# Hash attention and channel mix on one core: the projection load and two head loads change their DMA queues

## The chip, the cores and the metric

The kernel runs on one core of a Trainium2 chip. The metric is the device time of one execution in microseconds. Before the change the median of three runs is 248.6 us (248.2 to 249.51).

## The reference

The inputs are q, k and v (4 batches, 8 heads, 768 positions, 64 features, all float32), a projection of 64 x 6, and the weights of a channel mix. What is computed, cut to what matters:

```python
q_bits = (einsum('bhsd,dk->bhsk', q, proj) > 0)      # 6 bits for each position
k_bits = (einsum('bhsd,dk->bhsk', k, proj) > 0)
mask = q_bucket[:, :, :, None] == k_bucket[:, :, None, :]
scores = where(mask, q @ k.T / 8, -1e9)
attn = softmax(scores) @ v                           # x: [4, 768, 512] over all heads
xk = mu_k * x + (1 - mu_k) * x_prev                  # x_prev: x one position earlier
xr = mu_r * x + (1 - mu_r) * x_prev
out = sigmoid(xr @ w_r) * (relu(xk @ w_k)**2 @ w_v)
```

## The kernel before

The 32 heads are worked on as 16 pairs. For every pair there are 12 slots: 2 heads by 6 blocks of 128 keys. In a slot TensorE makes the scores of one key block against 768 queries (`score`, L484), ScalarE takes the exponential (L498), and two slots later TensorE multiplies it with the values (`pv`, L514). The bucket mask is put into the score as six extra rows of the operands: the signs of the projected q and k, written into `aq` and `ak` beside the 64 features. Between the score and the values of each slot stand the channel mix's matmuls of an earlier batch, and the preparation of later pairs. The whole order is written out by hand, with a table of work by pair and slot (`WORK`, `FETCH`); every engine carries out its own instructions in that order.

The start is what the change touches. It runs in this order in the code:

- L69: the projection (64 rows of 6 numbers, 1.5 KB) is loaded by GpSimd, ahead of the identities (`make_identity`) and of GpSimd's memsets (L221). L230 copies it on GpSimd to a second place, into partitions 64 to 127, when it has landed.
- `load_qk(0)` (L249 to L260) loads q and k of the first pair, one head at a time: head 0's q from SyncE, its k from ScalarE, then head 1's q from SyncE and k from ScalarE, 192 KB each.
- L955 and L956: a small activation on ScalarE, with which the activation table is loaded.
- From SyncE, in this order: v of head 0 (192 KB), q and k of pair 1 (`load_qk(1)`, L262, 384 KB each), two small loads of `mu_rows` (L960), v of head 1, v of pair 1, q and k of pair 2. The semaphores of loads are used again in turn, so that a later load on SyncE waits for one some eight loads earlier to land.
- `keep_warm(9, ...)` (L970): nine matmuls without use for the result.
- `turn_pe` (L326): three transposes on TensorE into a PSUM bank, then a copy to `t32` by VectorE (L333) or ScalarE (L335). The order on TensorE is: q of head 0, k of head 0, k of head 1 (L985, L986, L989), then the bit matmuls of head 0 (`bits_first`, L363; they need the projection, also its second place), q of head 1 (L994), q of pair 1's head 0 (L998), then the first score.
- `cast_pe` (L341) writes the features of q and k as bf16 into `aq` and `ak`, halves on VectorE, GpSimd and ScalarE. `signs_first` (L370) writes the signs: of q on ScalarE (L374), of k on VectorE (L403).
- Head 1's bit matmuls (`bits_of_second`) come in slot 0, after the first score.

Of the kernel before, what the change touches and what calls it, by code (L numbers as in the profile page):

```python
# [36 lines left out]
def kernel(  # L37
# [13 lines left out]
    nc = tc.nc  # L51
    B, H, S, D = q.shape
    NB = proj.shape[1]
# [10 lines left out]
    consts = ctx.enter_context(tc.tile_pool(name="consts", bufs=1))  # L64

    projp = consts.tile([P, 64], FP32, name="projp")
    nc.gpsimd.dma_start(out=projp[0:D, 0:NB], in_=proj)  # L69
    ident32 = consts.tile([P, P], FP32, name="ident32")  # L70
    make_identity(nc, ident32)
    ident16 = consts.tile([P, P], BF16, name="ident16")
# [99 lines left out]
    def fast():  # L172
        with ExitStack() as fx:
# [75 lines left out]
            def load_qk(n):  # L249
                b, t = divmod(n, NPB)  # L250
                tl = nat.tile([P, 2, 2, HALF], FP32, name=f"qk{n}", tag="qk")
                nats[n] = tl
                if n == 0:
                    for j in range(2):
                        for i, eng in enumerate((nc.sync, nc.scalar)):
                            eng.dma_start(  # L256
                                out=tl[:, i, j, :],
                                in_=SRC[i][b, 2 * t + j].rearrange("(p c) d -> p (c d)", c=NC_),
                            )
                    return  # L260
                for i in range(2):
                    nc.sync.dma_start(  # L262
                        out=tl[:, i, :, :],
                        in_=SRC[i][b, 2 * t : 2 * t + 2].rearrange(
                            "j (p c) d -> p j (c d)", c=NC_
                        ),
                    )
# [18 lines left out]
            def load_pair(n, sides="qk"):  # L286
                if n < NTE:
                    load_qk(n)
                else:
                    load_blocks(n, sides)  # L290
# [660 lines left out]


            load_qk(0)
            warm = rcp.tile([P, 1], FP32, name="warm", tag="warm")
            nc.vector.memset(warm, 0.0)  # L955
            nc.scalar.activation(warm, warm, AF.Exp)  # L956
            load_v(0, (0,))
            load_qk(1)
            for x, src in enumerate((moe_mu_k, moe_mu_r)):
                nc.sync.dma_start(  # L960
                    out=mu_rows[x * NDC : (x + 1) * NDC, :],
                    in_=src.rearrange("(c p) -> c p", p=P),
# [317 lines left out]
```

## Time and profile before

| | |
|---|---|
| median of 3 runs | 248.6 us |
| the profiled execution's own time | 248.52 us |
| its span, first to last instruction | 246.3 us |
| TensorE matmuls busy | 240.4 us, 98% |
| ScalarE busy | 208.4 us, 85% |
| VectorE busy | 176.5 us, 72% |
| GpSimd busy | 115.5 us, 47% |
| data moved by DMA | 36.70 MB |

Lines in the profile name the kernel's line (L331), the engine, the operation, what it writes and reads, and how many of them. PE is a matmul on TensorE, PEld a weight load on it, DVE VectorE, ACT ScalarE, POOL GpSimd, SP SyncE; a q behind the name means the engine's queue, where DMAs are issued. In a timeline the first column is the start in us, the second the length, and the bracket at the end says how long the engine was idle before and what ended that. Lines of stretches give, after the window, the busy time of each engine, then the granted clock of TensorE, the busy share of the DMA engines, and GB/s.

### The profile page before, as it was taken

Reading aid. Unit: us, or ns where it says so; the run is one execution under the profiler, and the core shown is the slowest. Engines: PE = TensorE matmul, PEld = TensorE weight load, DVE = VectorE, ACT = ScalarE, POOL = GpSimd, SP = SyncE. Lnnn points to the kernel's source line nnn. Section 1 sums busy time; section 2 is a strip of 40 time slices with the busy share of each in tenths; the row PEclk is TensorE's granted clock in tenths of the full one; section 3 lists DMA queues with packets and bytes.
Section 4 is the critical chain, followed back from the end, with each engine's and each line's share of the span. In section 5 each row is a group of like instructions: output and inputs, shape, how many; then the busy total and the mean of one; then the engine's idle time right before and its main releaser. Section 6 shows DMA issues by size and latency. Waiting matters only on the chain.

```text
span 246.3 us, 6710 instructions
## 1 busy us (share of the span) xinstructions
PE 240.4 (98%) x2443; PEld 145.6 (59%) x2443; DVE 176.5 (72%) x415; ACT 208.4 (85%) x344; POOL 115.5 (47%) x216
## 2 busy tenths in 40 slices
PE   8999999999999999999999999999999999999995
PEld 5566766665656556565665556565665656555443
DVE  2877887878887948586696957586696838499522
ACT  4898999999999989889999988889999999629620
POOL 6889786797637190835528091744619000000000
PEclk9999999999999999999999999999999999999999
DMA  6979888496999383956929475865920111120133
GB/s 219 373 173 243 175 192 195 80 224 166 201 205 232 108 199 97 271 119 207 185 72 212 106 197 134 244 134 173 214 71 5 48 45 43 45 86 3 43 115 107
DMA packets 28230, 36.70 MB, mean 149 GB/s; under 512 B 3216, under 2 KB 25376, under 8 KB 28192
## 3 DMA queue, kind: packets, MB, share of 16 engines
q1 hardware_dynamic: 25744, 33.21, 51.3%
q0 software_dynamic: 2160, 2.62, 7.0%
q8 instruction: 20, 0.33, 0.6%
q10 hardware_dynamic: 288, 0.39, 0.5%
q14 instruction: 18, 0.15, 0.2%
HBM read 31.99 MB, written 6.29 MB: 155 GB/s over the span
## 4 chain that ended last, share of the span: by engine, by line
PE 87%; ACT 7%; DMA 2%; issue 1%; SPq 1%; DVE 0%; ACTq 0%
PE sc L491 23%; PE vp L620 17%; PE kp L620 16%; PE oo L528 12%; PE rp L620 8%; ACT pt L498 6%; PE bb L450 3%; DMA qk<-in_q_dram 2%; PE ot L575 2%; PE tp L331 2%; PE oo L519 1%; PE bb L423 1%; ACT sq L314 1%; ACT kr L651 0%; SPq L256 0%
## 5 line engine op out<-in xcount | busy, mean ns | idle before, releaser
L498 ACT ACTIVATE pt<-sc 128x768 bf16<-128x768 f32 x192 | 151.1, 815 | 15.0 <-PE sc L491 12.4
L491 PE MATMUL sc<-aq,ak 70*128 70x384 bf16 (+1 forms) x384 | 93.8, 325 | 1.2 <-ACT pt L498 0.5
L528 PEld LDWEIGHTS <-pt 128*128 128x128 bf16 x1152 | 60.6, 97 | 27.0 <-ACT pt L498 0.2
L528 PE MATMUL oo<-va,pt 128*128 128x65 bf16 x1152 | 66.3, 193 | 0.0
L620 PE MATMUL vp<-wv_sb,k 128*128 128x512 bf16 (+1 forms) x200 | 54.4, 370 | 0.0
L620 PE MATMUL kp<-xk,wk_sb 128*128 128x384 bf16 x256 | 52.8, 326 | 0.2 <-ACT kr L651 0.2
L491 PEld LDWEIGHTS <-ak 70*128 70x128 bf16 (+1 forms) x384 | 34.3, 98 | 27.0 <-issue 4.6
L393 POOL TENSOR_SCALAR aq<-t 64x768 bf16<-64x768 f32 x24 | 19.9, 829 | 59.9 <-DVE t L388 45.8
L657 DVE TENSOR_TENSOR k<-kr 128x384 bf16<-128x384 bf16 x64 | 28.7, 458 | 11.7 <-ACT kr L651 11.2
L620 PEld LDWEIGHTS <-wk_sb 128*128 128x128 bf16 x256 | 21.6, 97 | 13.6 <-issue 3.8
L651 ACT ACTIVATE kr<-kp 128x384 bf16<-128x384 f32 x50 | 25.0, 499 | 4.5 <-PE kp L620 4.5
L620 PE MATMUL rp<-wr_sb,xr 128*128 128x512 bf16 x96 | 27.7, 379 | 0.0
L678 DVE SCALAR_TENSOR_TENSOR os<-th,vp 128x512 f32<-128x512 bf16 (+1 forms) x25 | 16.5, 661 | 15.0 <-PE vp L620 13.0
L620 PEld LDWEIGHTS <-k 128*128 128x128 bf16 x200 | 16.8, 97 | 10.8 <-issue 1.2
L668 ACT ACTIVATE th<-rp 128x512 bf16<-128x512 f32 x24 | 14.3, 595 | 9.8 <-PE rp L620 9.8
L388 DVE STREAM_TRANSPOSE t<-bl 128x768 f32<-128x768 f32 x24 | 22.3, 955 | 0.0
L393 POOL TENSOR_SCALAR ak<-t 64x768 bf16<-64x768 f32 x24 | 20.2, 840 | 4.3 <-DVE t L388 1.4
L479 POOL TENSOR_TENSOR s<-vf 128x192 f32<-128x192 f32 x32 | 20.7, 648 | 0.0
L314 ACT ACTIVATE sq<-bl 128x768 bf16<-128x768 f32 x24 | 20.2, 843 | 0.0
L576 DVE COPY xt<-ot 128x768 bf16<-128x768 bf16 x16 | 8.9, 558 | 14.3 <-PE ot L575 14.3
L477 POOL CAST va<-vf 128x384 bf16<-128x384 f32 x32 | 17.5, 548 | 2.5 <-DMA vf<-in_v_dram 1.6
L541 DVE TENSOR_TENSOR su<-oo,vb 128x390 f32<-128x390 f32 x12 | 6.7, 561 | 10.0 <-PE oo L528 10.0
(87 smaller groups left out, 238.5 us busy)
## 6 DMA issues: line engine op xcount, KB each, us to landing
bl<-in_q_dram SPq DMA_DIRECT2D x48, 176.0 KB
bl<-in_k_dram SPq DMA_DIRECT2D x48, 176.0 KB
vf<-in_v_dram SPq DMA_DIRECT2D x15, 384.0 KB
out_dram<-os SPq DMA_DIRECT2D x18, 256.0 KB
out_dram<-os SPq DMA_DIRECT2D x12, 128.0 KB
qk<-in_q_dram SPq DMA_DIRECT2D x3, 384.0 KB
qk<-in_k_dram SPq DMA_DIRECT2D x3, 384.0 KB
wk_sb<-in_moe_w_k_dram POOLq DMA_DIRECT2D x2, 512.0 KB, 6.9
```

The costliest lines, as they stand in the source:

```text
L314: nc.scalar.activation(junk, src, AF.Square, accum_out=acc)
L388: nc.vector.transpose(t32(n)[:, i].rearrange("p h (c f x) -> p (h c) f x", c=3, f=4), src)
L393: eng.tensor_scalar(out=augs[n % NSET]["qk"[i], j][ROWS[j], :], in0=t32(n)[ROWS[j], i].rearrange("p h y -> p (h y)"), scalar1=(1.0, ALPHA)[i],
L477: nc.gpsimd.tensor_copy(to, of)
L479: nc.gpsimd.tensor_add(s3, vf[:, 0 : 3 * D], vf[:, 3 * D : 6 * D])
L491: nc.tensor.matmul(sc[:, sp, 0:HALF], au["k", j][kr, jc * P : (jc + 1) * P], au["q", j][kr, sp * HALF : (sp + 1) * HALF], start=True, stop ...
L498: nc.scalar.activation(pt.rearrange("p (s q) -> p s q", s=2), sc[:, :, 0:HALF], AF.Exp, bias=EXP_BIAS, scale=SCALE / 2.0 if (n, j) == TWIC ...
L528: nc.tensor.matmul(oo[:, ic, :], pts[n, j, jc][:, ic * P : (ic + 1) * P], vas[n % NSET][j][:, jc, :],  start=(late(n) and jc == 0 and ic = ...
L620: nc.tensor.matmul(box["t"], lhs(), rhs(), start=(i == 0), stop=(i == len(mms) - 1))
L651: nc.scalar.activation(kr, kp, AF.Relu)
L657: 1, lambda: nc.vector.tensor_tensor(out=k2, in0=kr, in1=kr, op=ALU.mult)
L678: nc.vector.scalar_tensor_tensor(out=box["os"][:, y], in0=box["th"][:, y], scalar=1.0, in1=vp, op0=ALU.add, op1=ALU.mult,)
```

## The change

The projection is loaded by ScalarE, as its first load, and no longer by GpSimd. The loads of head 1 of the first pair change places: ScalarE loads its q and SyncE its k. Head 0 stays as it is, but its k is now ScalarE's second load. No other line changes; what is computed is the same.

```diff
     projp = consts.tile([P, 64], FP32, name="projp")
-    nc.gpsimd.dma_start(out=projp[0:D, 0:NB], in_=proj)
+    nc.scalar.dma_start(out=projp[0:D, 0:NB], in_=proj)
     ident32 = consts.tile([P, P], FP32, name="ident32")
...
                 if n == 0:
                     for j in range(2):
-                        for i, eng in enumerate((nc.sync, nc.scalar)):
+                        for i, eng in enumerate(((nc.sync, nc.scalar), (nc.scalar, nc.sync))[j]):
                             eng.dma_start(
                                 out=tl[:, i, j, :],
                                 in_=SRC[i][b, 2 * t + j].rearrange("(p c) d -> p (c d)", c=NC_),
```

## The prediction

> **What bounds the kernel now.** I read the page first: busy times and the chain that ended last.
>
> ```profile
> PE 240.4 (98%) x2443; PEld 145.6 (59%) x2443; DVE 176.5 (72%) x415; ACT 208.4 (85%) x344; POOL 115.5 (47%) x216
> PE 87%; ACT 7%; DMA 2%; issue 1%; SPq 1%; DVE 0%; ACTq 0%
> ```
>
> The end is set by TensorE's in-order stream, with some ScalarE exponentials in it. The 2% of DMA is one stretch at the very start, and the change touches only the start. So I opened the chain in order of time for the first 9 us.
>
> ```profile
> 2.13 5.59 DMA qk<-in_q_dram
> 7.72 0.14 issue
> 7.86 0.52 PE tp L331 x3
> 8.37 0.33 PE sc L491 x2
> ```
>
> Nothing before 7.72 us is TensorE work on this chain. TensorE waits for q of the second pair (`load_qk(1)`), whose turn (L998) stands ahead of the first score in program order. From 7.86 us on the chain is TensorE and ScalarE, with no DMA to hold it at a fixed time. So whatever moves the first score moves the end by the same amount, unless something else gets in first. The timeline gives the order of the start.
>
> ```profile
> 0.74 0.90 ACTq L256 DMA_DIRECT2D qk<-in_k_dram  x2
> 0.74 0.87 SPq L256 DMA_DIRECT2D qk<-in_q_dram  x2
> 1.28 0.74 POOL L69 DMA_DIRECT2D projp<-in_proj_dram  x1 [0.84 <-POOLq L1264]
> 1.67 1.28 ACT L956 ACT_TABLE_LOAD   x1 [1.67 <-PEq L1264]
> 2.96 0.20 ACT L956 ACTIVATE warm<-warm 128x1 f32<-128x1 f32 x1
> 3.64 0.92 PEld L331 LDWEIGHTS tp<-ident,qk 128*128 128x128 f32 x4 [0.23 <-issue]
> 4.79 0.48 ACT L335 COPY t<-tp 128x384 f32<-128x384 f32 x1 [1.62 <-PE tp L331]
> 5.31 0.39 POOL L230 COPY projp<-projp 64x6 f32<-64x6 f32 x1 [0.92 <-DMA projp<-in_proj_dram]
> 5.43 0.48 ACT L335 COPY t<-tp 128x384 f32<-128x384 f32 x1 [0.16 <-PE tp L331]
> 6.00 0.10 PEld L363 LDWEIGHTS bf0q<-t,projp 64*32 64x32 f32 x1 [0.17 <-issue]
> 6.78 0.55 PE L331 MATMUL tp<-ident,qk 128*128 128x128 f32 x3
> 6.95 0.99 ACT L374 ACTIVATE aq<-bf0q 6x384 bf16<-6x384 f32 x2
> 7.58 0.56 DVE L333 COPY t<-tp 128x384 f32<-128x384 f32 x1
> 7.86 0.52 PE L331 MATMUL tp<-ident,qk 128*128 128x128 f32 x3 [0.53 <-DMA qk<-in_q_dram]
> 8.21 0.49 PE L491 MATMUL sc<-aq,ak 70*128 70x384 bf16 x2
> 8.63 0.85 PE L363 MATMUL bf<-t,projp 64*32 64x384 f32 x8
> ```
>
> Two chains run to the first score. One is arithmetic: turns of q and k of head 0 (from 3.64 us), ScalarE's two copies (to 5.91), the bit matmuls (6.00), the two sign steps on ScalarE (6.95 to 7.94). The other is the load of `qk1`, which ends 7.72. The projection is on neither by a little: its copy ends 5.70, while k's copy, which the bit matmuls also need, ends 5.91.
>
> **The change part by part.** First, the projection leaves GpSimd. That takes 0.74 us of issuing off GpSimd; identities and memsets come 0.74 earlier. The identity was ready long before the first turn and the projection copy was 0.2 us early, so by itself this is worth nothing. It frees GpSimd at about 3.7 us instead of 5.70, which lets its casts of head 0 run when their inputs arrive; none of them is what ended last.
>
> Second, ScalarE issues three DMAs instead of two. One issue costs 0.90/2 = 0.45 us. The table load then starts about 2.12 and the warming step ends about 3.6; ScalarE's first copy comes at 4.79 after 1.62 us of idle time, so 0.45 us is covered with 1.2 to spare. Without that cover it would cost the 0.45 in full.
>
> Third, k of head 0 is issued one place later. When does it land, and when is it needed? SyncE's wait for it shows the first: the load of `mu_r` waits for k to land, and goes out at 3.75.
>
> ```profile
> 3.75 0.26 SPq L960 DMA_DIRECT2D mu_rows<-in_moe_mu_r_dram  x1
> SPq L960 <- DMA qk<-in_k_dram: 0.2, 1, 0.2
> 14.03 0.84 SPq L437 DMA_DIRECT2D aq<-sg  x1
> ```
>
> The fourth weight load of the turns is k's first; four of them end at 3.64 + 0.92 = 4.56, the last one takes about 0.23, so k is needed at about 4.33. Slack 0.58 us. The cost of an issue of 64 rows of 24 bytes on ScalarE is in no row; the rows of small transfers bound it at 0.26 (`mu_r`) and 0.84 us (a sign transfer). I take 0.45, the row of the same engine at the same time: k lands at 4.2, in time, price nothing. At 0.84 it lands at 4.6 and the second turn, the bits and the signs all slip by 0.26.
>
> Fourth, head 1. Its k moves to SyncE's second place (issue 1.19 as before, on the other queue) and its q to ScalarE's third (about 0.45 later than now). Its q is turned at 6.78, last of the four.
>
> ```profile
> 4.05 1.14 SPq L296 DMA_DIRECT2D vf<-in_v_dram  x2
> SPq L296 <- DMA qk<-in_k_dram: 0.4, 1, 0.4
> 5.23 0.47 SPq L262 DMA_DIRECT2D qk<-in_q_dram  x1
> ```
>
> SyncE's second v load waits for ScalarE's second load, which ends that wait at about 4.8 (4.05 + 1.14 less one issue of 0.4). A third load in that queue lands one issue later, 5.2 to 5.3: 1.5 us before it is needed. Queued behind this wait on SyncE are v of pair 1 and q and k of pair 2; they go out up to 0.45 later, into a queue that still has pair 1's q and k, 768 KB, in front, so nobody waits for that.
>
> Fifth, and the one part that can move the end: when does q of pair 1 land? The same five 192 KB loads stand ahead of it as now, and the engines share them.
>
> ```profile
> 1.75:2.25 0.50, 0.50 (x3) 0.21 (x2) 0.50 (x14) 0.50 (x1) 0.50 (x3) 1.00 0.85 184
> 2.25:2.50 0.25, 0.25 (x2) 0.15 (x1) 0.04 (x5) 0.25 (x1) 0.23 (x2) 1.00 0.86 276
> 4.25:5.25 1.00, 1.00 (x6) 0.74 (x4) 0.00 (x0) 0.46 (x1) 0.14 (x1) 1.00 0.80 242
> 5.25:6.00 0.75, 0.75 (x5) 0.51 (x4) 0.35 (x1) 0.56 (x3) 0.54 (x4) 1.00 1.02 317
> 6.00:7.50 1.50, 1.32 (x12) 0.46 (x11) 0.51 (x1) 1.35 (x4) 1.42 (x3) 1.00 1.03 375
> projp<-in_proj_dram POOLq DMA_DIRECT2D x1, 1.5 KB, 3.9
> ```
>
> Last column GB/s. The rate falls to 242 between 4.25 and 5.25 us, although SyncE's queue holds over half a megabyte. In just that stretch the projection, the only transfer of GpSimd's software queue so far, arrives (issue 1.28 + 3.9 = 5.18). Against 375 GB/s the dip lacks 133 KB, and 5.25 to 6.00 another 43 KB: 176 KB / 375 = 0.47 us. If the projection's software descriptors make the dip, it goes, and q of pair 1 lands up to 0.47 sooner. Against that, k's later issue leaves the engines with one queue for 0.45 us while they are not full (184 and 276 GB/s): at most half of the traffic there, 0.45 x 230 / 2 = 52 KB, 0.14 us. So the landing moves by between -0.47 and +0.14 us. I take -0.4: nothing else in the trace coincides with the dip.
>
> What is late next? The signs: the score's second matmul needs the last one, 7.94. Now that matmul ends at 8.21 + 0.49 = 8.70 after the turn; with the turn done earlier it would start at about 7.98 and end at 8.31. The cap is 0.39 us. Behind it the bits of head 1 need VectorE's copy, which ends 8.14: no obstacle. So the first score moves by about 0.3 to 0.4; I take 0.3, a tenth lost on the way because ScalarE's queue between signs and first exponential stays full.
>
> The sum: 0 (GpSimd) + 0 (ScalarE's issue) + 0 (k, q of head 1) - 0.3 = span 246.0, and the profiled time of 248.52 (2.2 us over its span) becomes 248.2. The median of the runs, 248.6, is 0.1 above the profiled time and becomes 248.3. A measurement of this kernel can tell about 0.5%, 1.24 us, from no change (the three runs alone reach from 248.2 to 249.51), so I call this no change.
>
> **The rivals.** (1) Nothing moves. The dip may be the loads' own, whatever its cause; then q of pair 1 lands as before or up to 0.14 later. Time 248.6 to 248.75. For it: the projection is 1.5 KB, against 176 KB missing. Against it: the coincidence in time. The Trainium skill, "DMA: Bandwidth & Descriptors", section "Issuing engines are not separate DMA queues", speaks for this rival: all queues run on the same 16 engines and a second issuer saves only issuing time. By that rule the sum would be 248.6. The trace agrees in that both queues together move no more (378 GB/s, the row below) than SyncE's alone later on (375, above):
>
> ```profile
> 2.50:3.00 0.50, 0.50 (x4) 0.20 (x2) 0.00 (x0) 0.49 (x2) 0.50 (x3) 1.00 1.06 378
> ```
>
> (2) k is late. With an issue of 0.84 us and the projection's rows slow in front of it on the same queue (up to 0.5 us more, an estimate from the dip) k lands at 5.1, 0.8 after its need; turns, bits and signs slip by as much, the signs end at 8.7, and the score's second matmul ends at 9.1 instead of 8.70: +0.4, 249.0. It decides from a landing beyond 4.33 + 0.4.
>
> (3) Slower: TensorE's clock opens later. Its matmuls show two speeds at the same granted 1.00.
>
> ```profile
> L972 PE MATMUL idle<-epsm x9: 499/524/524, 1.1 to 3.6; 128*128 128x384 bf16 x9
> L331 PE MATMUL tp<-ident,qk x48: 270/273/476, 3.9 to 29.0; 128*128 128x128 f32 x48
> L491 PE MATMUL sc<-aq,ak 70*128 70x384 bf16 x1 | 0.3, 327 | 0.0
> ```
>
> 384 columns take 524 ns at first and 327 at 8.2 us; the turns go from 476 to 273 between. So the array speeds up between 4 and 6.8 us, after some 4 us of nearly unbroken work. If k comes late, TensorE idles in just that time, and the speed-up could come some 3 us later. The work from 7.86 to about 9.5 (1.6 us on the chain) would then run at about half speed: +1.6 us, with k's own delay 250.2 to 250.6. It decides when TensorE's idle time before 5.8 us grows by over about half a microsecond. The Trainium skill, "TensorE: Matmul & The Clock Gate", "Part 1: The HAM clock gate", says that the gate judges activity in a free-running window of about 3.4 us; by that rule the moment also shifts between executions of one kernel, which one trace cannot show.
>
> (4) Faster by over 0.5%: the speed-up falls two microseconds earlier. The turns and bits from 3.91 to 5.8 then take about half, up to 0.9 us, and with the 0.4 of the load 247.3.
>
> **How the numbers follow.** Forecast 0.47, range 247.9 to 248.6. Rival 1: 0.20. Rival 2: 0.13. These three are all within 0.5%: 0.80. Rival 3: 0.10. Rival 4: 0.10, with the scatter of the runs in both. The likeliest gives 248.3. The range takes in the first three with the runs' scatter of some 0.4 us at the lower end and 0.2 at the upper: 247.5 to 249.2; rivals 3 and 4 are left out, 2 in 10.
>
> **What would show it.** GB/s between 4.25 and 5.25 us at 350 or more (else the dip was not the projection's). The turn of `qk1` before 7.5 us and the first score's second matmul ending by 8.4. The wait of TensorE at 7.86 for q replaced by one for ScalarE's signs. k of head 0 landed by 4.3, seen in the second copy of L335 still starting at 5.43; the bits at 6.00. The table load at about 2.1. The prediction is wrong if the second copy slips by over 0.3 us, if turns still take over 400 ns after 6 us, or if a wait for a load shows later than 9 us on the chain.

## The result, and the profile after

The change makes the kernel slower: median 250.18 us (nine runs, 249.75 to 251.53) against 248.5 us (nine runs of the kernel before, 248.19 to 249.51), ratio 1.0064 with a 95% interval of 1.0051 to 1.0078. The forecast was 248.3 us and no change. The profiled execution took 249.96 us, its span is 248.0 us (before: 246.3). Of all runs below, one of `g1_swap_delay` (254.54 us) was in a slower state of the chip; the ratios leave it out, and without it that kernel's median is 248.69.

The page of the kernel after, busy TensorE and the shares of the chain that ended last:

```profile
PE 240.6 (97%) x2443; PEld 145.2 (59%) x2443; DVE 176.9 (71%) x415; ACT 208.4 (84%) x344; POOL 114.8 (46%) x215
PE 84%; ACT 10%; DMA 2%; issue 2%; DVE 2%; ACTq 0%
```

The work is the same (240.6 us of matmuls, 240.4 before); what grew is waiting. The chain in order of time, start and length in us, names the place:

```profile
0.74 0.55 ACTq L68
1.32 4.64 DMA qk<-in_k_dram
5.96 0.04 issue
6.01 0.88 PE tp L331 x6
6.89 0.44 PE bf0q L363
```

Before, this chain began with SyncE's issues and the load of q of pair 1, up to 7.72. Now it begins with ScalarE's issue of the projection and goes through k of head 0, which lands at 5.96. The timeline of the kernel after, the lines that answer to those of before:

```profile
0.74 0.55 ACTq L68 DMA_DIRECT2D projp<-in_proj_dram  x1
1.32 0.60 ACTq L256 DMA_DIRECT2D qk<-in_k_dram  x1
1.95 0.45 ACTq L256 DMA_DIRECT2D qk<-in_q_dram  x1
2.43 1.28 ACT L956 ACT_TABLE_LOAD   x1 [2.43 <-issue]
3.58 0.18 POOL L229 COPY projp<-projp 64x6 f32<-64x6 f32 x1 [0.49 <-DMA projp<-in_proj_dram]
3.90 0.85 PE L331 MATMUL tp<-ident,qk 128*128 128x128 f32 x3
4.79 0.48 ACT L335 COPY t<-tp 128x384 f32<-128x384 f32 x1 [0.86 <-PE tp L331]
5.98 0.84 SPq L296 DMA_DIRECT2D vf<-in_v_dram  x2
6.01 0.88 PE L331 MATMUL tp<-ident,qk 128*128 128x128 f32 x6 [1.26 <-DMA qk<-in_k_dram]
6.60 0.48 ACT L335 COPY t<-tp 128x384 f32<-128x384 f32 x1 [1.33 <-PE tp L331]
7.13 0.10 PEld L363 LDWEIGHTS bf0k<-t,projp 64*32 64x32 f32 x1 [0.18 <-ACT t L335]
8.04 0.98 ACT L374 ACTIVATE aq<-bf0q 6x384 bf16<-6x384 f32 x2
8.78 0.62 PE L491 MATMUL sc<-aq,ak 70*128 70x384 bf16 x2
9.84 0.82 ACT L498 ACTIVATE pt<-sc 128x768 bf16<-128x768 f32 x1
15.07 0.84 SPq L437 DMA_DIRECT2D aq<-sg  x1
20.82 0.48 PE L491 MATMUL sc<-aq,ak 70*128 70x384 bf16 x2 [0.78 <-ACT pt L498]
```

ScalarE's second copy, of the turn of k, slips from 5.43 to 6.60, the bits of k from 6.00 to 7.13, the signs from 6.95 to 8.04. In the timeline of the kernel before, the first exponential and the first score of pair 1 stand at:

```profile
8.79 0.82 ACT L498 ACTIVATE pt<-sc 128x768 bf16<-128x768 f32 x1
19.07 0.48 PE L491 MATMUL sc<-aq,ak 70*128 70x384 bf16 x2
```

So the loss comes in two steps: 1.05 us at the first exponential (8.79 to 9.84; 0.99 at most of those behind it), and 1.75 from pair 1's first score on (19.07 to 20.82). From there every later exponential is 1.75 late, but for single ones, to the end. The second step stands on SyncE's queue. Its wait for k, in the view of SyncE's waits up to 9 us:

```profile
SPq L296 <- DMA qk<-in_k_dram: 1.8, 1, 1.8
```

The two v loads went out at 4.05 before and go out at 5.98 now; the bulk loads (L281, q of pair 4) and pair 1's sign transfers (L437) stand behind them in the same queue. In the kernel before, and then in the kernel after, the bulk loads go out and VectorE makes the signs at:

```profile
9.16 1.93 SPq L281 DMA_DIRECT2D bl<-in_q_dram  x4
12.98 1.02 DVE L403 TENSOR_SCALAR sg<-bb 128x384 bf16<-128x384 f32 x2 [0.29 <-PE bb L423]
```

```profile
9.46 2.95 SPq L281 DMA_DIRECT2D bl<-in_q_dram  x4
14.02 1.02 DVE L403 TENSOR_SCALAR sg<-bb 128x384 bf16<-128x384 f32 x2
```

The sign transfers go out at 15.07 instead of 14.03 because the signs are ready 1.04 us later; that is still the first step. What comes on top is the way from issue to landing: the first two of them, which pair 1's first score needs, have landed at 20.73 instead of 18.98, 5.66 us behind the first issue instead of 4.95. The bulk loads ahead of them have all landed at 20.30 instead of 18.40; by 12 us the DMA engines had moved 3.04 MB instead of 3.55. That the wait for k at 4 us set the queue back by this much fits these times, but no run takes that wait away alone. Before, TensorE came to the score without idle time, 0.09 us after they had landed, so they had next to no slack; now it idles for 0.78 us and starts 0.09 us after them. (The bracket of the score's line names ScalarE, which was done long before.)

The lines of stretches (last column GB/s) show that the dip of the prediction did not go away with the projection's software descriptors:

```profile
2.50:3.00 0.50, 0.50 (x4) 0.21 (x2) 0.00 (x0) 0.50 (x1) 0.50 (x2) 1.00 0.97 324
3.50:4.25 0.75, 0.75 (x4) 0.57 (x3) 0.00 (x0) 0.42 (x2) 0.33 (x3) 1.00 0.96 289
4.25:5.25 1.00, 0.50 (x3) 0.10 (x1) 0.00 (x0) 0.46 (x1) 0.00 (x0) 1.00 0.88 227
```

It is 227 GB/s, where it was 242; and from 2.5 to 4.25 us the engines, which moved 378 and 358 GB/s before, now move 324 and 289.

### The profile page after: what moved, and what is told of

The parts are those of the page before. It is cut to its first block, busy times and chain, and to the rows that moved or that the text cites. A ratio compares the mean times of both kernels' runs of the same rounds, so it can differ in the third digit from the quotient of the medians.

```text
span 248.0 us, 6710 instructions
## 1 busy us (share of the span) xinstructions
PE 240.6 (97%) x2443; PEld 145.2 (59%) x2443; DVE 176.9 (71%) x415; ACT 208.4 (84%) x344; POOL 114.8 (46%) x215
## 4 chain that ended last, share of the span: by engine, by line
PE 84%; ACT 10%; DMA 2%; issue 2%; DVE 2%; ACTq 0%
PE sc L491 22%; PE vp L620 17%; PE kp L620 16%; PE oo L528 12%; ACT pt L498 9%; PE rp L620 8%; PE bb L450 3%; PE ot L575 2%; DMA qk<-in_k_dram 2%; PE tp L331 1%; PE bb L423 1%; PE oo L519 1%; ACT sq L314 1%; DVE ak L403 0%; ACT kr L651 0%
## 5 line engine op out<-in xcount | busy, mean ns | idle before, releaser
L657 DVE TENSOR_TENSOR k<-kr 128x384 bf16<-128x384 bf16 x64 | 28.6, 457 | 11.7 <-ACT kr L651 11.2
L479 POOL TENSOR_TENSOR s<-vf 128x192 f32<-128x192 f32 x32 | 21.2, 662 | 0.0
L477 POOL CAST va<-vf 128x384 bf16<-128x384 f32 x32 | 17.0, 531 | 3.2 <-DMA vf<-in_v_dram 2.4
```

The source lines that it names most:

```text
L477: nc.gpsimd.tensor_copy(to, of)
L479: nc.gpsimd.tensor_add(s3, vf[:, 0 : 3 * D], vf[:, 3 * D : 6 * D])
L657: 1, lambda: nc.vector.tensor_tensor(out=k2, in0=kr, in1=kr, op=ALU.mult)
```

## Experiments

All ratios are to the kernel before, timed beside each of them. "k" is k of head 0; it has landed when the last of its 16 pieces has. One profile shows one execution, so a landing or a speed from it is one draw; the medians are over four to twelve runs. The table has the columns that the readings below use. Slow packets are the 1.5 KB packets on ScalarE's queue between 2.5 and 5.25 us that took over 0.3 us, where the median packet takes 0.065 us in every one of these kernels (counted in the trace's packet records). The last column is the time up to which TensorE's matmuls ran at half speed (a turn's matmul 421 ns instead of 273), and any later stretch in which they did so again. The trace also records TensorE's granted clock. That record begins, with 1.0, at 5.78 us in the kernel before and at 4.74 in the kernel after (TensorE was idle there from 4.75 to 6.01, so the 6.0 of the table is only its first fast matmul); the views print 1.00 ahead of its beginning too, although the matmuls are slow there, so that this 1.00 says nothing. A later stretch at half speed stands in the record as 0.5.

| kernel | median us | ratio [95%] | k landed | slow packets | half speed until |
|---|---|---|---|---|---|
| before | 248.5 | 1 | 3.73 | 1 | 5.6 |
| after | 250.18 | 1.0064 [1.0051, 1.0078] | 5.96 | 4 | 6.0 |
| e1_proj_only | 251.16 | 1.0101 [1.0079, 1.0123] | 6.30 | 8 | 13.3 |
| e2_swap_only | 248.67 | 1.0003 [0.999, 1.0015] | 3.65 | 1 | 3.6 |
| e3_proj_third | 248.73 | 1.0011 [0.9982, 1.0039] | 3.75 | 2 | 5.3 |
| e4_signs_gpsimd | 259.5 | 1.042 [1.0371, 1.047] | 5.58 | 8 | 3.9 |
| d1_delay_only | 251.18 | 1.0083 [1.0054, 1.0113] | 4.83 | 2 | 5.0; 8.0 to 11.6 |
| d2_wide_rows_first | 251.55 | 1.0117 [1.0088, 1.0147] | 5.85 | 4 | 3.6; 7.4 to 10.5 |
| g1_swap_delay | 248.83 | 1.0003 [0.9979, 1.0026] | 4.80 | 2 | 5.6 |
| g2_both_delayed | 249.42 | 1.0035 [1.0019, 1.0051] | 4.36 | 2 | 4.8 |
| f1_hold_sync | 249.6 | 1.0043 [1.0013, 1.0072] | 5.84 | 8 | 5.9 |
| f2_after_v_behind | 250.45 | 1.0055 [1.0025, 1.0085] | 5.60 | 14 | 9.9 |
| f3_before_v_behind | 249.09 | 1.0015 [0.9993, 1.0037] | 3.48 | 1 | 4.8 |
| f4_proj_second_v_behind | 249.2 | 1.0026 [1.0, 1.0052] | 3.68 | 1 | 5.6 |
| g3_after_split | 251.28 | 1.0094 [1.0075, 1.0114] | 6.65 | 6 | 13.0 |
| g4_before_split | 249.25 | 1.0027 [1.0013, 1.0041] | 3.69 | 0 | 5.5 |
| c1_after_blocks_later | 251.29 | 1.0114 [1.0064, 1.0163] | 6.22 | 8 | 9.5 |
| c3_third_blocks_later | 249.55 | 1.0032 [1.002, 1.0043] | 3.74 | 0 | 5.3; 8.9 to 12.1 |
| h1_four_rows_first | 248.96 | 1.0016 [0.9999, 1.0033] | 5.86 | 4 | 9.1 |
| h2_two_small_first | 252.07 | 1.0148 [1.0131, 1.0165] | 6.96 | 16 | 4.3; 7.8 to 11.2 |

### Which part of the change costs the time

The first alone: the projection is ScalarE's first load, head 1's loads stay as before.

```diff
-    nc.gpsimd.dma_start(out=projp[0:D, 0:NB], in_=proj)
+    nc.scalar.dma_start(out=projp[0:D, 0:NB], in_=proj)
```

> Half of the change: the projection is ScalarE's first load, head 1's loads stay as before (q SyncE, k ScalarE). Theory A (the projection's load ahead of k of head 0 on ScalarE's queue makes that k late; everything else follows): the whole loss, 250.0 to 250.3 us, the second turn at about 6 us. Theory B (the exchange of head 1's loads makes it, because SyncE's queue then brings k of head 1 while k of head 0 waits): nothing of it, 248.3 to 248.7 us, the second turn at 4.3 us. Both parts: something between.

The second alone: head 1's q and k change queues, the projection stays with GpSimd.

```diff
-                        for i, eng in enumerate((nc.sync, nc.scalar)):
+                        for i, eng in enumerate(((nc.sync, nc.scalar), (nc.scalar, nc.sync))[j]):
```

> The other half: head 1's q by ScalarE and k by SyncE, the projection by GpSimd as before. Theory A: no change, 248.3 to 248.8 us, k of head 0 landed by 3.8 us. Theory B: the loss, 249.5 to 250.3 us.

Both, but the projection is ScalarE's third load, behind k of head 0 and q of head 1; GpSimd's copy of it goes behind it in the code.

```diff
-    nc.scalar.dma_start(out=projp[0:D, 0:NB], in_=proj)
...
                     for j in range(2):
...
+                    nc.scalar.dma_start(out=projp[0:D, 0:NB], in_=proj)
```

> The change, but the projection is ScalarE's third load, behind k of head 0 and q of head 1. Theory A: k of head 0 is first again, so the loss goes: 248.3 to 248.7 us, unless the projection now comes too late for the bit matmuls at 6.0 us (it landed 2.7 us after its issue in the changed kernel; issued at 1.65 it lands near 4.4 to 5, in time). A rival (taking the projection off GpSimd's queue is itself what hurts, whatever its place): 249.5 or more.

The loss is the projection's place: ahead of k it costs 2.6 us alone (251.16), third it costs nothing that can be told (248.73). The swap alone is worth nothing (248.67), but beside the early projection it is worth about 1.0 us (251.16 to 250.18). The chain of e1 shows why:

```profile
1.33 0.60 ACTq L256
1.96 5.54 DMA qk<-in_k_dram
7.50 0.14 issue
7.63 0.87 PE tp L331 x3
8.51 0.78 PE bf0q L363
```

ScalarE's third load lands at 7.50. Without the swap that load is k of head 1, whose turn stands ahead of the bits; with it, it is q of head 1, which is turned after the bits. So the swap keeps the worst of the lateness off the path. The timeline of TensorE in e1 shows a second price, which the lateness brings with it:

```profile
6.35 0.90 PE L331 MATMUL tp<-ident,qk 128*128 128x128 f32 x3 [1.60 <-DMA qk<-in_k_dram]
7.63 0.87 PE L331 MATMUL tp<-ident,qk 128*128 128x128 f32 x3 [0.38 <-DMA qk<-in_k_dram]
9.87 1.54 PE L331 MATMUL tp<-ident,qk 128*128 128x128 f32 x6
```

Six turns take 1.54 us, where they take 0.88 in the kernel after. TensorE runs at half speed until 13.3 us in this execution; its record of the granted clock begins at 13.17. The kernel after paid none of that in its profile: its turns at 6.01 are already fast.

### Is it only that k is issued later?

The kernel before, with ScalarE's first load held back by a wait for a VectorE memset, to 1.32 us, where the change issues k; nothing stands ahead of it.

```diff
+            first_pair = nat.tile([P, 2, 2, HALF], FP32, name="qk0", tag="qk")
+            nc.vector.memset(first_pair[:, 1, 0, 0:1], 0.0)
```

> The kernel before, with a small memset by VectorE into the tile of k of head 0, so that ScalarE's first load waits until about 1.3 us, as late as behind the projection; nothing is loaded ahead of it and the projection stays on GpSimd. Theory D (issued 0.6 us later, k is overtaken by SyncE's loads and shares the engines with them): the whole loss of the projection-only kernel, 250.5 to 251.2 us, k landing at 5.5 to 6.3 us. Theory N (the 64 rows of 24 bytes hold up the engines or the queue): k lands about 0.6 us later than before, 4.3 us, and the time is 248.4 to 248.9 us.

The same with the swap:

> The kernel before with head 1's loads exchanged as in the change, and ScalarE's first load held until about 1.3 us by the small memset; nothing is loaded ahead of k and the projection stays on GpSimd. It is the changed kernel without the small load. Theory P (the 0.6 us of delay alone makes the loss): 249.8 to 250.4 us, as the changed kernel. Theory S (a small load ahead in the queue adds a loss of its own; with the delay alone k of head 0 landed at 4.83 us, behind a small load at 5.6 to 6.3): 248.9 to 249.4 us.

And both queues' first loads held back to 1.32 us (`first_pair[:, :, 0, 0:1]`), without the swap:

> The kernel before with the first loads of both queues, SyncE's q and ScalarE's k of head 0, held until about 1.3 us; everything behind them moves too. Theory P in its strong form (what counts is ScalarE's queue against SyncE's, not the time): all loads land 0.5 to 0.7 us later in the same order, the first score is as much later, 249.0 to 249.4 us, less than the 251.18 of the kernel that delays ScalarE's queue alone, although more is delayed. Rival M (a slow time of memory or engines between 3.5 and 6 us hits whatever is then on its way): k of head 0 after 5 us, head 1 after 6.5, 250.3 us or more.

With the swap the delay costs nothing: 248.83 us, ratio 1.0003. Its chain has k landing at 4.80:

```profile
1.32 3.48 DMA qk<-in_k_dram
4.80 0.14 issue
4.94 1.23 PE tp L333 x6
```

That is 0.6 us later than the turn of k stood before, but the first exponential is only 0.30 late, as the wait for q of pair 1 took up the rest. So in the changed kernel the issue time of the projection is not what costs: k issued at 1.32 lands at 4.80 with nothing ahead of it and at 5.96 with the projection ahead, and the difference of 1.16 us in landing goes with 1.35 us in the median (248.83 to 250.18; 1.49 from 248.69). The landings of single profiles bear it out: 5.58 to 6.65 us in the seven kernels with the projection first, 4.80 and 4.83 in the two with ScalarE's delay alone. Holding both queues back, so that they keep step, costs 0.9 us.

Without the swap the delay alone costs as much as the whole change and more, 251.18 us, but not through k of head 0. The load of k of head 1 in the chain of d1, and TensorE's timeline:

```profile
1.73 5.71 DMA qk<-in_k_dram
4.96 0.52 PE L333 MATMUL tp<-ident,qk 128*128 128x128 f32 x3 [0.20 <-DMA qk<-in_k_dram]
7.58 0.52 PE L333 MATMUL tp<-ident,qk 128*128 128x128 f32 x3 [2.10 <-DMA qk<-in_k_dram]
9.46 1.54 PE L333 MATMUL tp<-ident,qk 128*128 128x128 f32 x6
```

k of head 0 is hardly late; k of head 1, ScalarE's second load, lands at 7.45 and leaves TensorE idle for 2.10 us. In e1, with the projection ahead, the same load landed at 7.50. So without the swap the delay of the issue is enough for the whole loss of e1 (251.18 against 251.16), with no small load in the queue; with the swap ScalarE's second load is q of head 1, which is turned behind the bits. Of the two theories put down for d1, D had the time and neither had k's landing. Why 0.6 us of delay makes ScalarE's second load so late is not shown. The turns on both sides of this gap are fast (0.52), those at 9.46 slow again: the gap is followed by a stretch at half speed from 8.03 to 11.56, with a granted clock of 0.5 from 8.08 on. The Trainium skill, "TensorE: Matmul & The Clock Gate", "Part 1: The HAM clock gate", has a free-running window of about 3.4 us that judges activity; the clock records here agree, with one stretch of 3.41 us at 0.5 each in d1 (from 8.08), d2 (7.21), h2 (7.97) and c3 (8.86).

### What in a small load ahead of k makes it late?

A useless load of 64 rows of 512 bytes ahead of k on ScalarE's queue, in the kernel before (no swap, projection on GpSimd):

```diff
+    spare = consts.tile([P, P], FP32, name="spare")
+    nc.scalar.dma_start(out=spare[0:D, :], in_=q[0, 0, 0 : 2 * D].rearrange("(p c) d -> p (c d)", c=2))
```

> The kernel before, with one more load of no use ahead of k of head 0 on ScalarE: 64 rows of 512 bytes (32 KB); the projection stays on GpSimd. Theory D: the loss as with the projection's load, 250.5 to 251.5 us. Theory N (only narrow rows hurt): 248.5 to 249.0 us, k of head 0 landing by 4.5 us.

A useless load of 4 rows of 512 bytes in the same place, with the swap:

```diff
+    spare = consts.tile([P, P], FP32, name="spare")
+    nc.scalar.dma_start(out=spare[0:4, :], in_=moe_mu_k.rearrange("(c p) -> c p", p=P))
```

> The kernel before with two edits: head 1's q and k change queues as in the change, and a load of 4 rows of 512 bytes, which nothing uses, stands ahead of k of head 0 on ScalarE's queue; the projection stays with GpSimd. Theory A (any load ahead of k puts the 16 engines of that queue out of step, however few rows it has): k of head 0 lands at 5.6 us or later, 249.8 to 250.6 us. Theory B (it takes a load of many rows, spread over all engines, to delay the last of k's pieces): k lands at about 4.8 as with the delay alone, 248.5 to 249.2 us.

The changed kernel with the projection loaded twice ahead of k, the first time into a tile that nothing reads:

```diff
+    spare = consts.tile([P, P], FP32, name="spare")
+    nc.scalar.dma_start(out=spare[0:D, 0:NB], in_=proj)
```

> The changed kernel with the projection loaded twice, the first time into a spare tile that nothing uses: two loads of 64 rows of 24 bytes ahead of k of head 0 on ScalarE's queue. If each small load costs k the same again (5.96 against 4.80 us with the delay alone, so 1.2 us, or at the least its issue of 0.55 us), k lands at 6.5 to 7.2 us and the time is 250.8 to 252. If the loss is one of being out of step, and is had in full with the first small load, k lands at about 6.0 to 6.5 and the time stays at 250.0 to 250.6.

The width of the rows makes no difference that can be told: 512 bytes cost what 24 bytes do (251.55 against 251.16, both without the swap). A second small load costs more; k lands at 6.96 instead of 5.96, and the median grows by another 1.9 us:

```profile
1.97 4.99 DMA qk<-in_k_dram
6.96 0.04 issue
7.01 0.88 PE tp L333 x6
```

Of the 1.0 us in landing 0.65 is issue time (1.97 against 1.32); the other 0.35 is less than the profiles with one projection ahead differ among themselves (5.58 to 6.65), so that the second load stretches the transfer further is not shown. TensorE idles for 2.29 us and then runs at half speed from 7.82; that goes with the rest of the loss.

Four rows cost little: 248.96 us, within the bounds for a load that does no harm. But its profile is that of the slowest of its ten runs, 249.98 us, and in that one execution k landed late after all:

```profile
1.33 4.53 DMA qk<-in_k_dram
5.86 0.04 issue
5.90 1.54 PE tp L333 x6
```

The turns are slow there too. Both theories put down for this kernel hold in part: by the median few rows make it rarer, by the profile not impossible. What the other nine runs looked like inside no profile shows.

### Is it competition from SyncE's queue, or the size of its transfers?

SyncE's third load (v of head 0) held back to 2.35 us in the changed kernel, by a wait for a VectorE memset:

```diff
+            vfs[0] = vfp.tile([P, 2, S // 2], FP32, name="vf0", tag="vf")
+            nc.vector.memset(vfs[0][:, 0, 0:1], 0.0)
```

> The changed kernel, with SyncE's third load (v of head 0) and all behind it held back until about 2.3 us by a small memset by VectorE, 0.65 us later than in the changed kernel, so that ScalarE's late loads again stand to SyncE's as they did before. Theory D (k is late because SyncE's loads get in first and share the engines): k of head 0 lands by 4.7 us, q of head 1 by 5.8, q of pair 1 at 8.3 to 8.5; the first score is then 0.6 to 0.8 late and the time 249.1 to 249.5 us, faster than the changed kernel although three loads more start late. Rival M (the memory side is slow between 3.5 and 6 us, whoever loads): k of head 0 still lands after 5.3 us, 250.2 us or more.

v of head 0 moved behind q of pair 1, in the changed kernel, in the kernel before, and in the changed kernel with the projection as ScalarE's second load (behind k):

```diff
+                    if (n, i) == (1, 1):
+                        load_v(0, (0,))
...
-            load_v(0, (0,))
```

> The changed kernel with v of head 0 behind pair 1's q on SyncE's queue, so that 384 KB of pair 1's q take the place of 192 KB of v as what competes with ScalarE's loads. Theory D: k of head 0 and q of head 1 land as late as in the changed kernel or later (6 and 7.3 us), 250.0 to 250.8 us. Rival V (the first touch of v in memory slows the engines): k of head 0 lands by 5 us and the time is below 249.7 us.

> The kernel before with only that move: v of head 0 behind pair 1's q. The first score waits for pair 1's q (7.72 us) and the last sign is done at 7.94; v is needed on GpSimd at 7.0 and on TensorE at 11. If the order in which loads reach the engines is what counts: q of pair 1 lands at 7.1 to 7.3, the first score is 0.2 to 0.4 us earlier, 248.2 to 248.4 us. If k or q of head 1 lands later because the longer transfer competes earlier: 248.6 us or more.

> The projection as ScalarE's second load, behind k of head 0 and ahead of q of head 1, head 1 exchanged as in the change, and v of head 0 behind pair 1's q. k of head 0 is first again, and lands at 3.75. The projection lands by 5 us. Theory D: ScalarE's third load, q of head 1, is the late one (6.5 to 7.4 us), wanted at 6.8: 248.2 to 248.9 us. If a small load on ScalarE's queue hurts wherever it stands: 249.5 or more.

q and k of pair 1 in four transfers of 192 KB instead of two of 384, in the changed kernel and in the one before:

> The changed kernel with q and k of pair 1 in four transfers of 192 KB instead of two of 384 KB. If an engine's turns between the queues go by whole transfers (a late load waits behind 16 rows of pair 1's q instead of 8): q of head 1 lands by 6.5 us instead of 7.33 and the time falls to 249.2 to 249.8 us. If turns do not depend on the transfer's size: 250.0 to 250.5 us.

> The kernel before with the same split. The first score's turn then waits for half of pair 1's q only, which should land at about 6.9 instead of 7.72 us; the last sign is done at 7.94: the first score up to 0.35 us earlier, 248.1 to 248.4 us. If the gain is given back at pair 1's first score, which waits for sign transfers behind the bulk loads: 248.5 to 248.9 us.

None of it brings k forward by much. Held back, SyncE's third load lets k land at 5.84 instead of 5.96:

```profile
1.32 4.52 DMA qk<-in_k_dram
5.84 0.04 issue
5.88 0.88 PE tp L331 x6
```

The median falls by 0.6 us, in intervals that overlap, and f2 gains nothing. Splitting pair 1 makes the changed kernel slower (251.28) and the one before a little (249.25). So neither the order of SyncE's loads from the third on nor the size of its transfers is what delays k. SyncE's first two loads stand beside k in all these kernels, so competition from them is not tested. f4, with the projection second, is at 249.2 us (f3, with the same move of v and the projection on GpSimd, at 249.09): behind k the small load costs at most a few tenths.

What the runs do have in common stands in the table's column of slow packets. Wherever a small load stands ahead of k on ScalarE's queue there are 4 to 16; wherever none does, delayed or not, there are 0 to 2. In the kernel after, 15 of k's 16 pieces have landed by 4.85 us and the last at 5.96; the slowest packet of ScalarE's queue starts at 4.30 and takes 1.23 us. That fits a load that is complete only with its last piece, held up by single packets of 1.5 KB that take up to 20 times as long as the median one, but it is argued, not shown: a packet's record names its queue and not its load, and in e1 and f1 five of the 16 pieces came after 5 us, not one. Nor are slow packets special to a small load: SyncE's queue has 2 to 10 of them in the same stretch, ten in the kernel after and ten in g1. Why a small load ahead brings them to ScalarE's queue is not shown.

### Can the second step be taken away?

Pair 1's sign transfers from GpSimd's queue, in the changed kernel:

```diff
-            BY_GPSIMD = ()
+            BY_GPSIMD = (1,)
```

> The changed kernel, with pair 1's four sign transfers issued by GpSimd on its own queue instead of SyncE, where they stand behind the bulk loads. The exponentials are 0.99 us late from the first slot on and 1.75 late from pair 1's first score (19.7 us). Theory C (the second step of 0.75 is the sign transfers, which land late behind the loads on SyncE's queue): the step goes, 249.3 to 249.6 us. If the second step is only the first one carried on by another wait: 250.0 to 250.3 us.

Pair 4's q load moved from slot 0 to slot 5, out of the way of the sign transfers, in the changed kernel and in e3:

```diff
                 (0, 0): (
                     lambda: load_pair(3, "qk"),
-                    lambda: load_pair(4, "q"),
                 ),
                 (0, 5): (
                     lambda: load_v(2),
+                    lambda: load_pair(4, "q"),
                 ),
```

> The changed kernel, with the load of q of pair 4 (704 KB in four transfers, first used in pair 2) moved from slot 0 to slot 5, behind pair 1's sign transfers on SyncE's queue. Theory C (the second step of 0.75 us, at pair 1's first score, is the sign transfers landing late behind the bulk loads): the step goes, 249.2 to 249.6 us. If the step has another cause: 250.0 to 250.3 us.

> The projection as ScalarE's third load (its profile had the first score 0.33 us earlier and then 1.05 us lost at pair 1's first score, which waited for the sign transfers), with the same move of pair 4's q behind those transfers. Theory C: the loss at pair 1 goes and the first 0.33 us is kept, 248.0 to 248.4 us, with less spread between runs. Rival (the gain at the start is given back anyway): 248.5 to 248.9 us.

No. GpSimd issues the signs behind its own casts and sums, which its chain shows:

```profile
20.24 0.68 POOL aq L437
20.93 6.21 DMA ak<-sg
```

It issues them at 20.24 us, 5 us later than SyncE, and pair 1's first score, at 27.23, is 8.2 us later than in the kernel before. With pair 4's load moved, c1's exponentials are 2.0 us late both ahead of pair 1 and at its first score: the step there is gone, which bears out that pair 4's loads in SyncE's queue made it. But a step of 1.5 us appears at pair 2's first score, and the median is 251.29. In e3 the profiled execution has a step at pair 1 too, although its first score is on time; TensorE's timeline there:

```profile
20.13 0.48 PE L490 MATMUL sc<-aq,ak 70*128 70x384 bf16 x2 [1.42 <-DMA ak<-sg]
```

Its signs went out at 13.71, 0.32 us earlier than in the kernel before, and by 12 us as much had been moved (3.53 MB against 3.55), yet the second of the two transfers landed at 20.04 instead of 18.98. So pair 1's signs, which have next to no slack in the kernel before, are a second place where small shifts become time, and a longer wait of SyncE at 4 us is not the only thing that makes them late. Moving pair 4's load in e3 gained nothing either: c3 is at 249.55 against 248.73. Its profile, the slowest of its eight runs (252.46), shows that the third place is not free in every execution: the projection landed at 7.53, and TensorE idled 1.8 us for it ahead of the bits.

## Why the prediction was wrong

**What held.** The parts on GpSimd and on ScalarE's issue were right. The projection is copied at 3.58 and nobody waits for it; ScalarE's first copy starts at 4.79 as before, after 0.86 us idle. The table load came at 2.43 (2.1 foretold), since the issues took 0.55, 0.60 and 0.45 us instead of 0.45 each. The place was right as well: the first 9 us, and the order of arrivals there.

**The step that failed: part three, k of head 0.** It put the landing at 4.2 us, "in time, price nothing", by adding the issue time of the projection to a landing of 3.75, and bounded it at 4.6. The landing was 5.96. The mistake was to take the load's transfer time as fixed and to move only its start. From issue to landing k took 2.99 us before, 3.48 when only its start moved (g1, where it cost nothing: 248.83 us), and 4.64 behind the projection: what stands ahead in the queue, and what else is under way by then, belong to the price.

**Rival 2 had the mechanism, with too small a size.** "k is late" foresaw 5.1 us and 249.0; the turn of k came 1.7 us after its need (6.01 against 4.33) instead of 0.8, which gave 1.05 us at the first exponential instead of 0.4.

**Part four: "so nobody waits for that".** SyncE's v loads went out 1.93 us later, after a wait of 1.8 us for k, not up to 0.45 later. The prediction followed the queue only as far as pair 2's loads; behind those, pair 4's q was 1.90 us late in landing and pair 1's signs 1.75, of which 1.04 is the first step. The rest is the second step of 0.7 us. That the wait at 4 us is its whole cause is not shown; e3 has a step at the same place with the v loads at 4.84. The prediction's own signs of error came: the second copy slipped by 1.17 us, where 0.3 was its limit, and TensorE waited for a transfer beyond 9 us, at 20.82. q of head 1 landed at 7.33, 2 us later than foretold, and had no price since the swap puts it behind the bits.

**Part five: the dip.** It was the only term with a gain, and it did not exist. The software descriptors are gone and the rate between 4.25 and 5.25 us is 227 GB/s instead of 242. A coincidence in time was taken for a cause: g1, whose projection GpSimd still loads, moves 350 GB/s in that stretch, and c3, whose projection ScalarE loads, 226. Rival 1 doubted it rightly. The Trainium skill, "DMA: Bandwidth & Descriptors", "Issuing engines are not separate DMA queues", says that another issuer saves only issue time; that rate agrees with it. k's landing, which moved with the company it has in its queue, is not covered by it. What makes the dip stays open.

**Rival 3, the slower TensorE,** was not the cause in the profile of the kernel after (six turns at 6.01 in 0.88 us, and a clock record that begins at 4.74). That the median of 250.18 us lies beside this rival's 250.2 is chance. The prediction read the two speeds as lying at the same granted 1.00; the change of speed at 5.8 us is where the clock's record begins, at 5.78. But the mechanism is real: in e1, d1, d2 and h2 a late load left TensorE idle for 1.5 to 2.3 us and half speed followed or stayed. It goes with losses larger than the lateness of the loads. A later stretch of 3.41 us at 0.5 shows in a run's mean granted clock, 0.993 in the profiles of d1, d2, h2 and c3. That mean is on record for every run, and 0.993 stands in one of nine runs of the kernel after (250.19 us), in three of four of e1, four of ten of d1, three of four of h2 and none of ten of h1. So it was rare in the kernel after; a first speed-up that comes late, as in e1's profile, leaves no mark in the mean, and how often that struck cannot be told.

**Rival 4, the earlier speed-up,** can be answered from e2: its clock record begins at 3.71 us, 2.07 earlier than in the kernel before, and the run took 248.73 us. Its chain goes through the load of q of pair 1, which landed at 8.04; while that load comes last, faster turns ahead of it gain nothing.

**Settled and open.** Settled: in the changed kernel the projection ahead of k on ScalarE's queue is the loss, through k's landing; the delay of its issue alone is not, though without the swap it is enough (d1); the swap takes about 1 us off the loss. Open: why k's transfer is stretched, whether single slow packets do it, and whether the number of the small load's rows counts (h1's median points there, its profile speaks against it); and what set the queue back at pair 1's signs.

## What to carry to other kernels

When a small load is put ahead of a large one on a queue, do not price it by its issue time alone: look at when the last piece of the large load lands, and put the small one behind it if it can wait (and see when it lands itself: 7.53 us, too late, in the profile of c3). When a wait on a queue grows, follow everything behind it in that queue to the first consumer that has no slack, here, it may be, a score 15 us later. A gain that rests on a coincidence of two things in time needs an experiment that takes one of them away before it counts as a term.

## What the runs showed of the hardware that was not expected

A single 1.5 KB packet, 0.065 us in the median, can take 1.2 us or more (1.23 on ScalarE's queue in the kernel after, 1.56 on SyncE's in g3), and a load of 192 KB is complete only with its last piece (in the kernel after 15 of 16 had landed by 4.85 us, the last at 5.96). On ScalarE's queue, packets over 0.3 us between 2.5 and 5.25 us came in numbers of 4 to 16 where a small load stood ahead of k and of 0 to 2 where none did. And a gap of 2.10 us without matmuls (d1), or of 1.8 us (c3), was followed by 3.41 us at a granted clock of 0.5, while one of 1.26 us in the kernel after was not.
